# Attention scores of the later batches: three float16 products of split operands instead of one float32 product

## The chip, the cores and the metric

The kernel runs on one core of one Trainium2 chip. Its time is what the device takes for one execution, in microseconds (us). The core has TensorE for matrix products (in the profile PE, and PEld for its weight loads), VectorE (DVE), ScalarE (ACT), GpSimd (POOL) and SyncE (SP, which here only issues transfers). They run side by side, each through its own list of instructions in a fixed order, and wait for each other by semaphores.

## The reference

Windowed attention with 32 global tokens, and behind it a feed-forward layer on all 4608 tokens. Cut to what matters:

```python
# batch 8, heads 8, 512 local and 32 global tokens, head size 64
s_g = scale * q_g @ concat(k_g, k_l).T            # global queries see every key
s_ll = where(abs(i - j) <= 32, scale * q_l @ k_l.T, -1e9)
a_l = softmax(concat(scale * q_l @ k_g.T, s_ll))  # softmax subtracts the row's maximum
out = concat(softmax(s_g) @ v, a_l @ v)           # v = concat(v_g, v_l)
x = out.transpose(0, 2, 1, 3).reshape(4608, 512)
h = x @ w_in                                      # 512 x 2048
return (h * tanh(softplus(h))) @ w_out            # 2048 x 512
```

All inputs and outputs are float32. The queries and keys are drawn with a spread of about 0.57 to 0.8.

## The kernel before

**Attention.** The 8 heads of a batch are handled as 4 pairs; a pair's two heads stand on partitions 0 to 63 and 64 to 127. One transfer brings a pair's tile `qk` (128 x 1344 float32): 512 query columns, and 832 key columns in which each of four blocks of 128 queries finds its own keys, its neighbours' edge keys and the 32 global keys side by side. A unit is (batch b, pair hp, query block t); 128 units run in order. `scores` (L727) makes the scores of two units at once, one matrix product for each unit and head, into two of the three PSUM buffers of ring `sc`: this document calls that a score group, and there are 64 of them, 8 in each batch. For the second pair of every two it adds the global queries' scores of both pairs (`qg`, L744, and `g_go`, L886 to L891, in the third `sc` buffer). From batch 2 on all of this is one group, which this document calls a large one: 2 of the 8 groups in a batch. `row_max` (L760) masks a unit's scores, scales them and takes the row maximum on VectorE, `expo` (L767) takes the exponential on ScalarE; then the probabilities are split into float16 high and low parts (`ph`), turned by transposing transfers (`pt`), and multiplied with the values (`pv`, L856, into `U`).

**Feed-forward.** The tokens go through in 17 blocks of up to 256. All its products are already three float16 products of high and low parts. Blocks 0 to 4 use plain products (`m1_mm` into the two PSUM buffers of ring `h`, `mish` on ScalarE, `g_hi` and `g_lo`, then `m2_mm` into `o`). Blocks 5 and later form the first layer from seven products of sums instead of eight (`st_step`, L1158); for it `s_make` (L1074 and L1097) builds sums of weights on VectorE once, in the time of the batches 1 to 3, through a scratch tile `t`.

**What sets the order.** Every step is a task with the engines it may run on, a duration, and the tiles it reads and writes. The class `Plan` plays the program through with these durations and then writes each engine's instructions in the order of its start times; a task with two possible engines goes to the one that takes it first. So a change of a duration, a tile or a constant moves instructions on all engines. `slot(u)` names the tasks around unit u: scores of unit u+1, probabilities of u, values of u-1 or u-2, and the feed-forward steps due at u (table `S1`).

**Tiles.** `qk` has four buffers for the batches 0 and 1 and two afterwards; when they are free, buffer 3 also holds the scratch `t`, and parts of the others take sums of weights.

Of the kernel before, what the change touches and what calls it, by code (L numbers as in the profile page):

```python
# [10 lines left out]
F32 = mybir.dt.float32  # L11
# [27 lines left out]
MASKED = -8.0e9  # L39
# [13 lines left out]
T2 = 128  # L53
T3 = 131
T4 = 135
QTWO = 2
VPOOL = 1

# [257 lines left out]
def attn_mish_kernel(ctx: ExitStack, tc: tile.TileContext, qk, vm, vg, qg, w1, w2, consts_in, out, w64):  # L316
# [23 lines left out]
    def rings(pool, *table):  # L340
        for tag, bufs, shape, dt in table:
# [5 lines left out]
          ("vgraw", 1, [128, 128], F32), ("qg", 2, [128, HP, 64], F32),  # L347
# [6 lines left out]
          ("wm", 2, [128, 1], F32), ("dg", 2, [128, 128], F32), ("dv", 1, [128, 128], F32), ("pg", 1, [128, 2], F32), ("c", 3, [128, 3], F32),  # L354
# [34 lines left out]
    QK = own("qk", 4, [128, SL + KW], F32, (QTWO * HP, 2))  # L389
# [10 lines left out]
    pl.ring("t", 1, lambda name, i: QK[3][:, :512], keys={0: ("qk", 3)})  # L400
# [319 lines left out]
    HALVED = 2  # L720
# [39 lines left out]
    def row_max(b, hp, t, h):  # L760
# [3 lines left out]
            out=half(P, h, w), in0=X[s][:, cols(t)], in1=mask[:, m0:m0 + w], scale=-SCALE, scalar=3.0e38, op0=ALU.add, op1=ALU.min,  # L764
            accum_out=X[nm]), r=[s, "consts"], w=[[P, h]] if h else (), new=[("nm", nm)] if h else [("P", P), ("nm", nm)])
# [134 lines left out]
    def g_max(b, hp):  # L900
# [870 lines left out]
```

## Time and profile before

| | |
|---|---|
| time, median of 3 runs (lowest, highest) | 895.84 us (894.86, 897.37) |
| the profiled execution's own time | 897.46 us |
| its span, first to last instruction | 895.7 us |
| PE busy | 864.5 us, 97% of the span |
| DVE busy | 703.5 us, 79% |
| ACT busy | 584.0 us, 65% |
| POOL busy | 118.3 us, 13% |

The span is what the trace covers; 1.8 us of the profiled time lie around it. An engine is busy while an instruction of it is in progress, so an engine with a share near 100% has no time left, and one with a lower share waits or has nothing to do. Scores of the batches 0 and 1 start before 205.4 us, those of batch 2 at 205.44, of batch 3 at 274.85, of batch 4 at 353.55; the last score group is at 722.42 us. What follows is feed-forward alone.

### The profile page before, as it was taken

The numbers are of one execution on the slowest core, as the hardware profiler recorded it, in microseconds if no ns is written. First come the engines' busy times: TensorE is split into PE (matmuls) and PEld (weight loads), VectorE is DVE, ScalarE is ACT, GpSimd is POOL, SyncE is SP. The second block draws the span as 40 slices with busy tenths as digits, with TensorE's granted clock in tenths as the row PEclk, the third lists the DMA queues.
The fourth block names the chain that finished last, engine by engine and source line by source line (L and its number), as shares of the span: only waits on it lengthen the run. The fifth ranks groups of instructions, "written<-read, shape, count | busy, mean of one in ns | idle before, by whom it ended". The sixth has DMA issues, their size and how long they took to land.

```text
span 895.7 us, 24348 instructions
## 1 busy us (share of the span) xinstructions
PE 864.5 (97%) x9844; PEld 640.0 (71%) x9844; DVE 703.5 (79%) x1806; ACT 584.0 (65%) x1297; POOL 118.3 (13%) x224
## 2 busy tenths in 40 slices
PE   2889999999999999999999999999999999999997
PEld 1657668676676767777777777677777777689996
DVE  6999967559999797888659765886569789987675
ACT  2677887458688876786557665666567665454442
POOL 6211320021023102111110201011111000000000
PEclk9999999999999999999999999999999999999999
DMA  9975236634896976687637663666645431000000
GB/s 364 354 251 181 62 82 119 124 88 90 168 207 117 192 121 150 130 152 119 136 79 143 111 169 61 135 138 122 116 98 114 84 75 37 1 25 2 25 26 25
DMA packets 194593, 107.26 MB, mean 120 GB/s; under 512 B 175024, under 2 KB 179440, under 8 KB 193456
## 3 DMA queue, kind: packets, MB, share of 16 engines
q1 hardware_dynamic: 184352, 83.61, 44.2%
q0 software_dynamic: 9264, 19.21, 7.3%
q10 hardware_dynamic: 864, 2.88, 0.9%
q8 instruction: 77, 1.26, 0.6%
q14 instruction: 36, 0.29, 0.1%
HBM read 49.04 MB, written 8.91 MB: 65 GB/s over the span
## 4 chain that ended last, share of the span: by engine, by line
PE 87%; DVE 8%; DMA 3%; ACT 1%; issue 0%; POOL 0%; DVEq 0%; SPq 0%; ACTq 0%
PE o L1253 32%; PE h L1158 24%; PE h L989 10%; PE s L740 6%; PE U L856 5%; PE o L1348 4%; DMA pt<-ph 2%; DVE W L554 2%; DMA vraw<-in_vm 2%; DVE W L552 1%; PE gu L940 1%; PE g L891 1%; DVE W L545 1%; DVE P L763 1%; PE hx L1348 1%; DVE vmx L638 1%
## 5 line engine op out<-in xcount | busy, mean ns | idle before, releaser
L1253 PE MATMUL o<-W,G 128*128 128x512 f16 x1344 | 314.3, 379 | 0.0
L1253 PEld LDWEIGHTS <-G 128*128 128x128 f16 x1344 | 123.3, 97 | 127.2 <-issue 2.0
L1158 PEld LDWEIGHTS <-W 128*128 128x128 f16 x2880 | 167.5, 98 | 17.6 <-issue 2.2
L772 ACT ACTIVATE P<-P,nm 128x192 f32<-128x192 f32 (+1 forms) x256 | 117.7, 461 | 28.9 <-DVE nm L763 28.4
L989 PE MATMUL h<-xh,W 128*128 128x256 f16 x640 | 113.2, 273 | 1.0 <-ACT EE L1035 1.0
L763 DVE CUSTOM_DVE_ANT_0 P<-s,consts 128x192 f32<-128x192 f32 (+1 forms) x256 | 88.7, 368 | 32.1 <-PE s L740 28.9
L989 PEld LDWEIGHTS <-W 128*128 128x128 f16 x960 | 91.6, 98 | 16.9 <-issue 3.9
L1158 PE MATMUL h<-xh,W 128*128 128x128 f16 x1056 | 96.0, 219 | 0.0
L1158 PE MATMUL h<-xl,W 128*128 128x128 f16 x528 | 90.8, 219 | 0.0
L989 PE MATMUL h<-xl,W 128*128 128x256 f16 x320 | 87.2, 272 | 0.0
L712 POOL DMA_DIRECT2D vc<-vf x81 | 41.5, 515 | 256.3 <-DVE vf L694 115.0
L789 DVE SCALAR_TENSOR_TENSOR ph<-P,ph 128x384 f16<-128x384 f32 (+1 forms) x112 | 65.4, 587 | 11.0 <-ACT ph L456 10.0
L1158 PE MATMUL h<-raw,W 128*128 128x128 f16 x1152 | 73.9, 219 | 0.0
L856 PEld LDWEIGHTS <-pt 128*128 128x128 f16 (+1 forms) x1536 | 59.8, 98 | 18.1 <-issue 7.3
L740 PE MATMUL s<-qk 64*128 64x192 f32 (+1 forms) x512 | 63.8, 369 | 0.0
L449 ACT COPY EE<-h 128x512 f32<-128x512 f32 x48 | 28.0, 582 | 48.2 <-PE h L1158 45.3
L456 ACT ACTIVATE ph<-P 128x448 f16<-128x448 f32 (+1 forms) x102 | 54.8, 543 | 5.2 <-DMA pt<-ph 4.9
L1187 ACT ACTIVATE EE<-EE,c 128x1024 f32<-128x1024 f32 x24 | 27.6, 1149 | 46.1 <-DVE EE L1184 46.1
L856 PE MATMUL U<-vc,pt 96*128 96x64 f16 x768 | 56.0, 192 | 0.0
L856 PE MATMUL U<-vf,pt 128*128 128x64 f16 x720 | 52.4, 193 | 0.8 <-DMA pt<-ph 0.8
L740 PEld LDWEIGHTS s<-qk 64*128 64x128 f32 x512 | 42.8, 190 | 10.8 <-issue 5.5
L458 DVE TENSOR_SCALAR G<-VX,c 128x1024 f16<-128x1024 f32 x24 | 18.1, 754 | 38.7 <-ACT VX L1187 38.7
(246 smaller groups left out, 1583.7 us busy)
## 6 DMA issues: line engine op xcount, KB each, us to landing
qk<-in_qk SPq DMA_DIRECT2D x32, 672.0 KB, 4.9
W<-in_w POOLq DMA_DIRECT2D x17, 512.0 KB, 7.6
out<-ob SPq DMA_DIRECT2D x33, 256.0 KB, 2.8
vraw<-in_vm SPq DMA_DIRECT2D x8, 1024.0 KB, 6.1
raw<-in_w POOLq DMA_DIRECT2D x10, 512.0 KB, 5.2
W<-in_w ACTq DMA_DIRECT2D x5, 512.0 KB, 7.8
pt<-ph SPq DMA_TRANSPOSE x112, 3.4
vc<-vgf POOLq DMA_DIRECT2D x28, 48.0 KB, 3.0
```

The costliest lines, as they stand in the source:

```text
L449: A.copy(dst, src)
L456: A.activation(out=dst, in_=src, func=AF.Copy, scale=c)
L712: stream(POOL, dma(kib), lambda: G.dma_start(dst(), src()), 512, r=[r], w=[w], new=new, table="dma")
L740: T.matmul(X[s[h]][:, cols(u)], X[qk][r, u * 128:(u + 1) * 128], X[qk][r, SL + OWN[u]:SL + OWN[u] + WIDTH[u]], start=True, stop=True)
L763: pl.add(DVE, 77 + 1.03 * w, lambda: V.tensor_tensor_reduce(out=half(P, h, w), in0=X[s][:, cols(t)], in1=mask[:, m0:m0 + w], scale=-SCALE, ...
L772: pl.add(ACT, 460, lambda: A.activation(out=half(P, h, w), in_=half(P, h, w), func=AF.Exp, bias=X[nm], scale=-1.0, accum_out=X[sums][:, t, ...
L789: pl.add(DVE, dve(n), lambda: V.scalar_tensor_tensor(p_part(X[ph], t, 1), p_src(X[P], t), PSC, p_part(X[ph], t, 0), ALU.mult, ALU.subtract ...
L856: T.matmul(X[u][:, t, h, :], X[pt][:k, p * 4 + (c * 2 + h if b < TURNED else h * 2 + c), :], X[vx][:k, t, vl, h * 64:(h + 1) * 64], start= ...
L989: T.matmul(X[h][:, f * TB:(f + 1) * TB], wh(i, wl)[:, off:off + 128], X[x][:, d, o:o + TB], start=(n == 0), stop=(n == 11))
L1158: T.matmul(X[h][:, c:c + 128], form(J + jj, wl)[:, off:off + 128], x(l, d), start=(p in (1, 2, 5) and c == 0 and n == 0), stop=(n == 5), s ...
L1253: T.matmul(X[o], gp(g, blk, i)[:, f, t * 128:(t + 1) * 128], wh(8 + i, wl)[:, f * 512:(f + 1) * 512], start=(turn == 0 and n == 0), stop=( ...
L1348: T.matmul(X[o][:, cols], a_form(a, jj, f), b_form(w, jj, f), start=(fresh and n == 0), stop=(n == 11), skip_group_check=True)
```

## The change

From batch 2 on (`HALVED = 2`) the scores, the global ones too, are made from float16 parts.

- The global queries move into the tile `qk`, which grows from 1344 to 1408 columns; the separate transfer and tile `qg` go.
- Each pair's `qk` tile of batches 2 to 7 lands in one single buffer (QK[0]). `qk_scale` adds up the absolute values along each partition of the query side (576 columns) and of the key side (832 columns) with two ScalarE passes into `qs`; then GpSimd takes the maximum over the partitions, and five small VectorE instructions make powers of two from it (`sq`). `qk_split` writes the scaled high parts (ScalarE or VectorE, whichever the plan finds free) and the low parts (VectorE) as float16 into a new tile `pa`, two buffers in the places of QK[1] and QK[3]. The three steps are named 5, 4 and 3 units ahead of the pair's first scores.
- A score group of two units is now 3 products (high x high, high x low, low x high) for each unit and head: 12 float16 matrix products with 12 weight loads, where there were 4 float32 ones. A large group adds 6 for the global keys and 12 for the local keys, where there were 2 and 4.
- The scale is taken back in `row_max` and, through a small tile `cg`, in the global softmax.
- `t` becomes a tile of its own; constants of the plan differ.

```diff
-MASKED = -8.0e9
+MASKED = -1.0e30
+QG = 64
+KO = SL + QG
+QTOP, QTINY = 2.0 ** 14, 2.0 ** -14
...
-T2 = 128
-T3 = 131
+T2 = 127
+T3 = 133
...
-QTWO = 2
+HALVED = 2
...
+KLOAD, KSCALE, KSPLIT = 5, 4, 3
...
-    QK = own("qk", 4, [128, SL + KW], F32, (QTWO * HP, 2))
+    QK = own("qk", 4, [128, KO + KW], F32, (HALVED * HP, 1))
...
-    pl.ring("t", 1, lambda name, i: QK[3][:, :512], keys={0: ("qk", 3)})
+    ts_ = own("t", 1, [128, 512], F32, None)
+    pl.ring("dv", 1, lambda name, i: ts_[0][:, :128], keys={0: ("t", 0)})
+    pl.ring("pa", 2, lambda name, i: halfwords(QK[2 * i + 1]).rearrange("p (a c) -> p a c", a=2), keys={0: ("qk", 1), 1: ("qk", 3)})
...
-    def g_load(b):
-        stream(DMA, dma(128), lambda: load(X["qg", b], qg[b]), 1024, new=[("qg", ("qg", b))])
...
+    SIDES = (slice(0, KO), slice(KO, KO + KW))
+
+    def qk_scale(b, hp):
+
+        k, p, m, q, s = ("qk", b, hp), ("pa", b, hp), ("qs", b, hp), ("q2", b, hp), ("sq", b, hp)
+        for i, c in enumerate(SIDES):
+            pl.add(ACT, act(c.stop - c.start) + 90, lambda i=i, c=c: A.activation(out=X[p][:, 0, c].bitcast(BF16), in_=X[k][:, c], func=AF.Abs, bias=0.0, scale=1.0,
+                                                                    accum_out=X[m][:, i:i + 1]),
+                   r=[k], w=[[m, i], [p, i]] if i else (), new=() if i else [("qs", m), ("pa", p)])
+        pl.add(POOL, 900, lambda: G.partition_all_reduce(X[q], X[m], 128, RED.max), r=[m], new=[("q2", q)])
+
+        def go():
+            x, y = X[q], X[s]
+            V.tensor_scalar(x, x, QTINY, 1.0 / QTOP, ALU.max, ALU.mult)
+            pow2(x)
+            V.reciprocal(y[:, 0:2], x)
+            V.scalar_tensor_tensor(y[:, 2:3], x[:, 0:1], -SCALE, x[:, 1:2], ALU.mult, ALU.mult)
+            V.tensor_scalar(y[:, 3:4], y[:, 2:3], -1.0, None, ALU.mult)
+        pl.add(DVE, 420, go, w=[q], new=[("sq", s)])
+
+    def qk_split(b, hp):
+        k, p, s = ("qk", b, hp), ("pa", b, hp), ("sq", b, hp)
+        for i, c in enumerate(SIDES):
+            n = c.stop - c.start
+            pl.add([(ACT, act(n)), (DVE, dve2(n))], 0, lambda e, i=i, c=c: scaled(e, X[p][:, 0, c], X[k][:, c], X[s][:, i:i + 1]), r=[k, s], w=[[p, i]])
+        for i, c in enumerate(SIDES):
+            pl.add(DVE, dve(c.stop - c.start), lambda i=i, c=c: V.scalar_tensor_tensor(X[p][:, 1, c], X[k][:, c], X[s][:, i:i + 1], X[p][:, 0, c], ALU.mult, ALU.subtract),
+                   r=[k, s, [p, i]], w=[[p, (i, 1)]])
+
+    THREE = ((0, 0), (0, 1), (1, 0))
...
+        three = THREE if b >= HALVED else (None,)
+        part = lambda b, hp, i: X["pa", b, hp][:, i] if i is not None else X["qk", b, hp]
+
         def go():
             for u in (t, t + 1):
-                for h in range(2):
-                    r = slice(h * 64, h * 64 + 64)
-                    T.matmul(X[s[h]][:, cols(u)], X[qk][r, u * 128:(u + 1) * 128], X[qk][r, SL + OWN[u]:SL + OWN[u] + WIDTH[u]],
-                             start=True, stop=True)
+                for n, x in enumerate(three):
+                    i, j = x or (None, None)
+                    for h in range(2):
+                        r = slice(h * 64, h * 64 + 64)
+                        T.matmul(X[s[h]][:, cols(u)], part(b, hp, i)[r, u * 128:(u + 1) * 128], part(b, hp, j)[r, KO + OWN[u]:KO + OWN[u] + WIDTH[u]],
+                                 start=n == 0, stop=n == len(three) - 1)
...
+            for m, x in enumerate(three):
+                i, j = x or (None, None)
+                for n in range(2):
+                    T.matmul(X[g][n * 64:n * 64 + 64, c * 256:c * 256 + 256], part(n, i)[:, SL:KO], loc(part(n, j), 2 * c), start=m == 0, stop=m == len(three) - 1)
...
-    BLK2 = 18.779
+    BLK2 = 22.636
...
-    LAGX = 16.978
+    LAGX = 18.906
...
-    PACE = 0.821
-    MORE = 2.517
+    PACE = 0.895
+    MORE = 1.553
...
-    LATER = 28
-    BOOST = 21.993
-    BOOST2 = -10.661
+    LATER = 27
+    BOOST = 12.408
+    BOOST2 = 0.356
...
+        if KSPLIT in ready:
+            qk_split(*ready[KSPLIT][:2])
+        if KSCALE in ready:
+            qk_scale(*ready[KSCALE][:2])
...
-        if load3 and t == 0:
-            qk_load(*n3)
+        if KLOAD in ready:
+            qk_load(*ready[KLOAD][:2])
```

Three places in the order of instructions. In the names, `s_2_2_0_0` is batch 2, pair 2, first two units, head 0; `nm` is a row maximum, `U_2_1` the values' product of pair 1, `h_3_2` chunk 2 of the first feed-forward layer in block 3.

TensorE at the score groups of batch 2, pairs 2 and 3, before the change:

```order
L740 MATMUL s_2_2_0_0_3253<-qk0_103 128x192
...
L856 MATMUL U_2_1_3165<-vf1_118,pt1_123 128x64
...
L989 MATMUL h_3_1_3198<-xh_1_1798,W_73 128x256
...
L989 MATMUL h_3_2_3295<-xh_1_1798,W_73 128x256
...
L740 MATMUL s_2_2_1_0_3315<-qk0_103 128x224
...
L740 MATMUL s_2_3_0_0_3438<-qk1_104 128x192
```

and with it:

```order
L779 MATMUL s_2_2_0_0_3376<-qk1_104 128x192
...
L898 MATMUL U_2_1_3317<-vf1_118,pt1_124 128x64
...
L779 MATMUL s_2_2_1_0_3422<-qk1_104 128x224
...
L898 MATMUL U_2_1_3317<-vf1_118,pt2_125 128x64
...
L779 MATMUL s_2_3_0_0_3482<-qk3_106 128x192
...
L936 MATMUL g_2_3_3484<-qk1_104 64x256
...
L1044 MATMUL h_3_2_3547<-xh_1_1826,W_73 128x256
```

Before, feed-forward chunks stand between the score groups; now three score groups follow each other with only products of values between them, and the next chunk (`h_3_2`) comes behind all three.

ScalarE at the same place, with the change:

```order
L814 ACTIVATE P1_76,sums_2_2_3401<-P1_76,nm_2_2_0_0_3396 128x192
...
L463 ACTIVATE qk3_106<-qk0_103,sq_2_3_3336 128x832
L814 ACTIVATE P2_77,sums_2_2_3401<-P2_77,nm_2_2_1_1_3439 128x224
...
L814 ACTIVATE P1_76,sums_2_2_3401<-P1_76,nm_2_2_3_1_3478 128x192
L463 ACTIVATE ph1_82<-P2_77 128x2x224
L1090 ACT_TABLE_LOAD
L1090 ACTIVATE EE_120<-h_3_0_3222,c_3_1982 128x512
```

The mish of chunk `h_3_0`, which frees the PSUM buffer that `h_3_2` needs, now stands behind all eight exponentials of pair 2 and a high part; before the change it stood ahead of them.

VectorE there, with the change:

```order
L805 ISA P2_77,nm_2_2_1_0_3418<-s_2_2_0_0_3376,consts_65,sq_2_2_3146 128x224
...
L1129 TENSOR_TENSOR t0_121<-t0_121,W_73 128x512
L831 SCALAR_TENSOR_TENSOR ph1_82<-P0_75,ph1_82 128x2x192
L805 ISA P2_77,nm_2_2_1_1_3439<-s_2_2_0_1_3377,consts_65,sq_2_2_3146 128x224
...
L805 ISA P0_75,nm_2_2_2_1_3461<-s_2_2_1_1_3423,consts_65,sq_2_2_3146 128x224
...
L703 SCALAR_TENSOR_TENSOR qk3_106<-qk0_103,sq_2_3_3336,qk3_106 128x832
...
L805 ISA P1_76,nm_2_2_3_1_3478<-s_2_2_1_1_3423,consts_65,sq_2_2_3146 128x192
```

The low part of the next pair's keys (L703, 832 columns) and sums of weights (L1129) now stand between the row maxima of pair 2. Of the 48 steps of L1074 (now L1129) 4 stood ahead of batch 2, 26 in it and 18 behind it; with the change 22, 17 and 9.

## Rows read from the trace of the kernel before

**Rows 1.** The page: the span, and the engines' busy time (share) and instructions.

```profile
span 895.7 us, 24348 instructions
PE 864.5 (97%) x9844; PEld 640.0 (71%) x9844; DVE 703.5 (79%) x1806; ACT 584.0 (65%) x1297; POOL 118.3 (13%) x224
```

**Rows 2.** Windows cut at batch starts: length, busy us of each engine (instructions), clock, DMA.

```profile
0.00:108.65 108.65, 85.00 (x739) 59.47 (x739) 98.04 (x272) 72.75 (x182) 34.78 (x62) 0.97 0.70 247
108.65:205.44 96.79, 96.60 (x906) 69.15 (x905) 63.22 (x190) 67.17 (x153) 12.68 (x25) 1.00 0.49 100
205.44:274.85 69.41, 69.41 (x695) 46.30 (x694) 66.69 (x188) 53.65 (x129) 11.53 (x22) 1.00 0.79 164
274.85:353.55 78.70, 78.06 (x823) 55.53 (x820) 68.04 (x192) 60.35 (x138) 10.40 (x21) 1.00 0.75 144
353.55:445.24 91.69, 91.69 (x1220) 69.19 (x1217) 70.78 (x191) 69.07 (x151) 17.74 (x36) 1.00 0.72 136
...
542.01:638.78 96.77, 96.77 (x1206) 70.13 (x1204) 69.62 (x191) 62.17 (x142) 12.81 (x25) 1.00 0.62 120
```

**Rows 3.** Timeline of PE around a plain score group: start us, us, instruction, count.

```profile
406.44 0.97 PE L740 MATMUL s<-qk 64*128 64x224 f32 x8
407.34 0.34 PE L1158 MATMUL h<-raw,qk 128*128 128x128 f16 x3
```

**Rows 4.** Timeline of PE around a large score group.

```profile
222.74 0.97 PE L740 MATMUL s<-qk 64*128 64x192 f32 x8
223.65 0.31 PE L744 MATMUL s<-qk,qg 128*64 128x32 f32 x4
223.78 1.06 PE L891 MATMUL g<-qk,qg 128*64 128x256 f32 x8
224.78 0.61 PE L1253 MATMUL o<-W,G 128*128 128x512 f16 x2
```

**Rows 5.** Timeline of PE, float16 products in a row.

```profile
410.39 2.75 PE L1253 MATMUL o<-W,G 128*128 128x512 f16 x12
412.98 1.50 PE L1158 MATMUL h<-raw,G 128*128 128x128 f16 x24
414.32 0.25 PE L856 MATMUL U<-vf,pt 128*128 128x64 f16 x3
```

**Rows 6.** Timeline of PE, one float32 record on the whole array.

```profile
52.27 0.59 PE L609 MATMUL rest<-W,dg 128*128 128x512 f32 x1
52.70 0.38 PE L610 MATMUL rest<-W,minus 128*128 128x512 f16 x1
```

**Rows 7.** Timeline of PEld: weight loads.

```profile
404.64 0.45 PEld L856 LDWEIGHTS <-pt 128*128 128x128 f16 x12
405.02 0.99 PEld L1253 LDWEIGHTS <-G 128*128 128x128 f16 x6
```

**Rows 8.** Groups of instructions: busy us, mean ns of one, idle before.

```profile
L1048 DVE SCALAR_TENSOR_TENSOR G<-EE,c,G 128x512 f16<-128x512 f32 x40 | 29.8, 748 | 0.5
L1196 DVE SCALAR_TENSOR_TENSOR G<-VX,c,G 128x1024 f16<-128x1024 f32 x24 | 30.7, 1280 | 0.4
L864 DVE TENSOR_SCALAR rs<-sums 128x8 f32<-128x8 f32 (+1 forms) x40 | 6.5, 165 | 3.4 <-ACT P L772 3.2
L456 ACT ACTIVATE vf<-vraw,sv 128x512 f16<-128x512 f32 x29 | 20.5, 714 | 0.4
L456 ACT ACTIVATE W<-W,sw 128x1024 f16<-128x1024 f32 x15 | 17.2, 1144 | 1.3 <-DVE W L615 1.2
L772 ACT ACTIVATION_READ_ACCUMULATOR P<-P,nm 128x1 f32 x256 | 48.1, 188 | 0.0
L1074 DVE TENSOR_TENSOR qk<-qk,W 128x512 f32<-128x512 f32 (+1 forms) x28 | 19.2, 685 | 0.2
```

**Rows 9.** Waits of one GpSimd transfer: total us, times, longest.

```profile
POOL vgg L712 <- PE gu L940: 128.3, 7, 42.2
```

**Rows 10.** Transfers: KB each, median us from issue to landing.

```profile
qk<-in_qk SPq DMA_DIRECT2D x32, 672.0 KB, 4.9
```

More of the change, by code (lines that the diff above doesn't have):

```diff
@@ L748, in scores @@
         one = both and b >= HALVED
-        pl.add(PE, 1970 if one else 1145 if both else 907, go, r=[qk] + ([("qg", b), ("qk", b, hp - 1)] if both else []),
+        tag = "pa" if b >= HALVED else "qk"
+        pl.add(PE, 1330 if one else 545 if b >= HALVED else 1145 if both else 907, go, r=[(tag, b, hp)] + ([(tag, b, hp - 1)] if both else []),
                new=[("sc", s[0]), ("sc", s[1])] + ([("sc", ("g", b, hp))] if one else []))
@@ L887, in g_go @@
     def g_go(b, hp):
-        q, g, k = ("qg", b), ("g", b, hp), [("qk", b, hp - 1 + n) for n in range(2)]
+        g, three = ("g", b, hp), THREE if b >= HALVED else (None,)
+        part = lambda n, i: X["pa", b, hp - 1 + n][:, i] if i is not None else X["qk", b, hp - 1 + n]
         for c in range(2):
-            for n in range(2):
-                T.matmul(X[g][n * 64:n * 64 + 64, c * 256:c * 256 + 256], X[q][:, hp - 1 + n, :], loc(X[k[n]], 2 * c), start=True, stop=True)
+            for m, x in enumerate(three):
+                i, j = x or (None, None)
+                for n in range(2):
+                    T.matmul(X[g][n * 64:n * 64 + 64, c * 256:c * 256 + 256], part(n, i)[:, SL:KO], loc(part(n, j), 2 * c), start=m == 0, stop=m == len(three) - 1)
     def g_scores(b, hp):
-        pl.add(PE, 1017, lambda: g_go(b, hp), r=[("qg", b)] + [("qk", b, hp - 1 + n) for n in range(2)], new=[("sc", ("g", b, hp))])
+        pl.add(PE, 1017, lambda: g_go(b, hp), r=[("qk", b, hp - 1 + n) for n in range(2)], new=[("sc", ("g", b, hp))])
     def g_rest(b, hp):
@@ L1478, in attn_mish_kernel @@
     NEXT1 = 4
-    NEXT2 = 17
+    NEXT2 = 18
     NU = B * 16
@@ L1504, in attn_mish_kernel @@
     splits = []
-    F0 = 41.356
-    FSTEP = 0.782
+    F0 = 41.301
+    FSTEP = 0.862
     SFREE = S1[(GLATE - 1) * NF + 4]
     forms = [(F0 + FSTEP * n, (n // 3, n % 3 + 1)) for n in range(12)]
-    forms = [(max(k, SFREE + 1 if PIECES[j * 3 + n - 1][0][0] == "G" else 16 * QTWO + 1 if PIECES[j * 3 + n - 1][0][0] == "qk" else 0), (j, n)) for k, (j, n) in forms]
+    forms = [(max(k, SFREE + 1 if PIECES[j * 3 + n - 1][0][0] == "G" else 16 * HALVED + 1 if PIECES[j * 3 + n - 1][0][0] == "qk" else 0), (j, n)) for k, (j, n) in forms]
     forms += [(S1[ST0 * NF - 4 + j] + 1, (j, 4)) for j in range(4)]
@@ L1534, in slot @@
         b, hp, t = bu if bu else (0, 0, -1)
-        n1, n3 = divmod(b * HP + hp + 1, HP), divmod(b * HP + hp + 1, HP)
-        load3 = bu and b >= HALVED and n3 > (HALVED, 3 if QTWO > HALVED else 1) and n3[0] < B
+        n1 = divmod(b * HP + hp + 1, HP)
+        ready = {k: x for k in (KLOAD, KSCALE, KSPLIT) for x in [unit(u + k)] if x and x[0] >= HALVED and x[2] == 0}
         mv1 = bu and b >= HALVED and n1[0] < B
```

60 lines of the change are left out of this document (32 added, 28 removed).

## The prediction

> **What bounds the kernel now.** I read the page's busy shares first: PE works in 97% of the span, and no other engine above 79% [rows 1]. That is a mean over stages, so I cut the span at the starts of the batches and read every engine in each window [rows 2]. In the first 108.65 us PE is idle for 23.7, while DVE works for 98.0. From there to the end of batch 6 PE has no gap to speak of: 96.60 of 96.79 us, 69.41 of 69.41, 78.06 of 78.70, then all. So in the 48 score groups that the change touches PE is the bound, and a microsecond taken from its list is one gained, as long as the others keep up. The same windows say how near they are. In batch 2 DVE is busy for 66.69 of 69.41 us (96%), in batch 3 for 68.04 of 78.70, in batch 4 for 70.78 of 91.69, in batch 6 for 69.62 of 96.77. ACT has 15.8 us free in batch 2 and 35 in batch 6. The batches that follow each other fastest have the least room, and the change gives every pair more work on DVE and ACT.
>
> **Taken from PE.** A plain group lasts 0.90 us (406.44 to 407.34) for 8 records of 192 and 224 columns [rows 3]. Float16 products of 512 columns follow each other every 0.216 us and those of 128 columns every 0.056 [rows 5], a line of 0.003 us plus 0.417 ns per column: 0.083 us for 192 columns, 0.096 for 224, 0.109 for 256. A float32 record of 512 columns took 0.43 us, two such passes [rows 6]; a float32 product is two records, so four passes. One head's passes come to 4 x (0.083 + 0.096) = 0.715 us, two heads one after the other to 1.43. The measured 0.90 lies below that, so the heads, each on its half of the rows, run side by side, and 0.185 us are filling and switching. With three passes, 3 x 0.179 = 0.537. If all of the 0.185 stays the group lasts 0.72 and the gain is 0.18; if none stays, 0.36. I take 0.12 of it, near three quarters: 0.66 us, a gain of 0.24.
>
> A large group is 0.91 + 0.13 + 1.00 = 2.04 us [rows 4]. The middle becomes about 0.10. The last part is 16 passes of 256 columns, 8 behind each other if two run side by side (0.87), plus 0.13; now 6 x 0.109 + 0.13 = 0.78. Sum 0.66 + 0.10 + 0.78 = 1.54, gain 0.50 (0.41 to 0.77 by the same two ends). Batches 2 to 7 have 36 plain and 12 large groups: 36 x 0.24 + 12 x 0.50 = **14.6 us off PE** (11.4 to 22.2), 2.4 in each batch.
>
> **More weight loads.** A plain group now has 12 loads. Where float16 products are short, loads start 0.032 us apart, though each shows about 0.1 us (12 from 404.64, the twelfth ending 0.45 later) [rows 7]: they overlap, 12 x 0.032 = 0.38 lies below 0.537, and I add nothing. The Trainium skill ("TensorE: Matmul & The Clock Gate", section "LDWEIGHTS (loading the stationary operand)") prices a load at columns / 1.2 ns, 107 ns for 128 columns; one behind the other, 12 would take an estimated 1.28 us and the group would be longer than today. The trace disagrees for loads on the whole array; no row shows float16 loads for one half of it, so loads in single file stay a rival below.
>
> **Added to ACT and DVE.** For each of 24 pairs ACT sums absolute values over 576 and 832 columns. By its rows (512 columns 714 ns, 1024 columns 1144 ns, reading a sum 188 ns [rows 8]) that is 0.77 + 0.98 + 2 x 0.188 = 2.1 us; the high parts are 1.75 where ACT makes them, as it does in 43 of 48. 3.7 us a pair. DVE forms the low parts, between its rows of 512 and 1024 columns (748 and 1280 ns [rows 8]) 0.81 + 1.08 = 1.9, and the scales, five small instructions at 165 ns [rows 8], 0.8: 2.7 us a pair. The small copy `cg`, one a pair, is inside these.
>
> In batches 4 to 7 this is hidden. Batch 6: PE 96.8 - 2.4 = 94.4 us, DVE 69.6 + 10.8 = 80.4, ACT 62.2 + 14.8 = 77.0. Batch 4: PE 89.3, DVE 81.6, ACT 83.9. Batch 3 has PE 76.3, ACT 75.2, and DVE 70, since there 8 sums of weights fewer (0.685 each [rows 8]) and one pair's low parts fewer weigh against the added work. That is tight; I take 0, with a bound in the rivals.
>
> **Where it is not hidden.** In batch 2 PE needs 69.4 - 2.4 = 67.0. DVE gets 66.7 + 5 x 2.7 (its own four pairs' parts and one made ahead) + 2.2 (low parts that now stand there), less 13 sums of weights (8.9) that the order moves ahead of batch 2, into a window where DVE is busy for only 63.2 of 96.8 us [rows 2]: 73.4. That is 6.4 more than PE has, if DVE never waits, and 9.5 at the 96% that it reached. The order shows where: three score groups with only values' products between them, the chunk `h_3_2` behind, whose PSUM buffer is freed by a mish that ACT does only after all exponentials of that pair and a high part, and those wait for row maxima with a low part and weight sums between them. I take a **stall of 8 us** in batch 2 (bounds 0, if PE's order leaves enough between, and 12.8, from 73.4 at 92%). ACT there needs 53.7 + 14.8 = 68.5, close behind DVE.
>
> **Waits and transfers.** The maximum over partitions stands in POOL's list, behind moves that wait for PE (128.3 us in 7 waits, the longest 42.2 [rows 9]). It is named four units ahead, about 17 us in batch 2, and the pair's scores would wait behind a late one. One landing buffer serves all pairs: transfer 4.9 us [rows 10], sums 2.1, maximum and scales about 1.4 (an estimate), high 1.75, low 1.9, 12.1 us in a row, against 69.4 / 4 = 17.4 us for a pair in batch 2 and 24 in batch 6. It fits, with less slack in batch 2. On SP the next load waits until the low part is done, with the transposes of `pt` queued behind it; that is part of the 8. The bytes loaded stay the same (704 KB a pair for 672, and no `qg`). The start and the feed-forward tail behind the last group have the same work; 0, by 2 or 3 either way.
>
> **Sum.** 897.5 (the profiled execution's own time) - 14.6 + 8 = 890.9, 6.6 less. The profiled execution lies 1.6 above the median of the runs, so against 895.84: **889 us**.
>
> **Rivals.** About 0.3%, 2.7 us, is what a measurement of this kernel can tell from no change.
> - *Forecast* (0.47): 884 to 893, stall of 3 to 12.
> - *Nothing stalls, or the groups come near pure passes* (0.18): 895.8 less 14.6 to 20, 876 to 882. For it: ACT and DVE have free time in all batches from 4 on, and early steps of batch 2 could slip ahead. Against: 73.4 against 67.0.
> - *The stalls eat the saving* (0.19): 12 to 17 us of stall in batches 2 and 3, 893.2 to 898.5. For it: batch 3's ACT at 75.2 of 76.3.
> - *DVE and ACT become the bound* (0.13), the case on the other side: they wait for each other in a chain (maximum, exponential, high, low), so neither fills its time. At 92%: batch 2 lasts 73.4 / 0.92 = 79.8 (12.8 over PE), batch 3 75.2 / 0.92 = 81.7 (5.4), batch 4 83.9 / 0.92 = 91.2 (1.9): 20.1 less 14.6 is 5.5 slower, 901. It decides when these stalls pass 17.3 us, at a fill of about 93%. For it: ACT never worked over 77% of a batch when DVE was at 96%. Against: DVE did reach 96%, with PE never idle.
> - *Weight loads in single file* (0.03): 12 x 0.10 + 0.12 = 1.32 us a plain group, 0.42 more than now (36 x 0.42 = 15); a large one has 30 loads, 3.0 us, 1.0 more (12): 895.8 + 27 without any stall, 923 or later. The Trainium skill's price for a load, named above, would bring about this.
>
> **Range and chances.** 877 to 901 takes in the forecast, most of the first rival, all of the second and half of the third. Faster by over 0.3%: the forecast and the first, 0.65. Within: 0.19. Slower: 0.13 + 0.03 = 0.16. The forecast's own range is 884 to 893.
>
> **What would show it.** In the changed profile: plain groups of 0.66 us and large ones of 1.54 (the PE term); PE idle in batch 2 by about 8 us, around pairs 2 and 3, with waits of `h` chunks for the mish and of row maxima in DVE's list behind; DVE over 92% there; in batches 4 to 7 PE without gaps, and each some 2.4 us shorter; ACT up by about 80 us in all and DVE by 65. Wrong would be: a group of 0.9 us or more (loads), idle PE in batch 4 or later (ACT, or a late maximum on POOL), scores waiting for `pa` (the landing chain), or a changed tail.

## The result and the profile after

The changed kernel takes 905.56 us (904.16 to 906.78, 4 runs) where the kernel before took 896.12 (894.86 to 897.37): ratio 1.0105, 95% interval 1.0083 to 1.0127. It is 9.4 us slower; 6.6 us faster was forecast. The profiled execution took 904.16.

The page of the changed kernel, span and busy time, beside [rows 1]:

```profile
span 902.3 us, 25249 instructions
PE 856.3 (95%) x10108; PEld 633.3 (70%) x10108; DVE 766.9 (85%) x1987; ACT 657.2 (73%) x1446; POOL 125.1 (14%) x248
```

PE is busy for 8.2 us less and the span is 6.6 longer, so its idle time grew by 14.8: 2.8 of it before batch 2, 11.7 in batches 2 to 4. Windows of the changed kernel, cut at the batch starts as in [rows 2] (the first two are batches 0 and 1; an engine's idle time is the length less its busy time):

```profile
0.00:98.27 98.27, 71.67 (x648) 50.37 (x648) 87.11 (x253) 64.63 (x172) 27.16 (x51) 1.00 0.75 267
98.27:207.38 109.11, 109.11 (x1008) 77.26 (x1008) 86.86 (x233) 78.94 (x180) 19.30 (x39) 1.00 0.45 91
207.38:287.58 80.20, 71.76 (x740) 48.82 (x740) 73.29 (x216) 66.14 (x153) 12.27 (x25) 0.91 0.76 146
287.58:370.42 82.84, 79.88 (x904) 56.73 (x902) 71.24 (x204) 66.82 (x153) 13.15 (x26) 0.98 0.68 131
370.42:460.91 90.49, 89.50 (x1227) 66.35 (x1226) 82.61 (x230) 81.88 (x179) 16.86 (x34) 1.00 0.74 140
460.91:555.32 94.41, 94.35 (x1249) 68.25 (x1249) 79.48 (x212) 76.24 (x168) 13.52 (x28) 1.00 0.64 126
555.32:650.12 94.80, 94.67 (x1250) 68.34 (x1250) 81.57 (x230) 76.84 (x170) 14.50 (x30) 1.00 0.61 125
```

Stage by stage in us, with the forecast's own terms:

| | batches 0, 1 | 2 | 3 | 4 | 5 | 6 | 7 and tail | span |
|---|---|---|---|---|---|---|---|---|
| before | 205.4 | 69.4 | 78.7 | 91.7 | 96.8 | 96.8 | 256.9 | 895.7 |
| forecast | 205.4 | 75.0 | 76.3 | 89.3 | 94.4 | 94.4 | 254.5 | 889.3 |
| after | 207.4 | 80.2 | 82.8 | 90.5 | 94.4 | 94.8 | 252.2 | 902.3 |

From batch 4 on the forecast holds to 1.2 us a batch. Batch 2 is 5.2 longer than forecast, batch 3 is 6.5, the start 2.0; batch 7 and the tail are 2.3 shorter. Some of this is work that the new order moved: PE's list in batch 3 now holds 12 more products into `o`, 48 more of 128 columns and 24 fewer of 256, at the intervals of the prediction an estimated 2.7 us more, and behind batch 6 there are 11 products into `o` fewer.

PE at a plain and at a large score group of the changed kernel in undisturbed batches, beside [rows 3, 4]:

```profile
508.25 0.71 PE L779 MATMUL s<-qk 64*128 64x192 f16 x12
508.89 0.26 PE L898 MATMUL U<-vf,pt 128*128 128x64 f16 x3
...
529.62 0.71 PE L779 MATMUL s<-qk 64*128 64x192 f16 x12
530.26 0.27 PE L785 MATMUL s<-qk 128*64 128x32 f16 x6
530.37 0.82 PE L936 MATMUL g<-qk 128*64 128x256 f16 x12
531.13 0.26 PE L898 MATMUL U<-vf,pt 128*128 128x64 f16 x3
```

From start to start a plain group takes 0.64 us (0.66 forecast), a large one 0.64 + 0.11 + 0.76 = 1.51 (1.54 forecast).

PE in batch 2 of the changed kernel, rows with idle time (in brackets, with what ended it) and two of a chunk:

```profile
244.08 0.71 PE L779 MATMUL s<-qk 64*128 64x192 f16 x12
245.28 0.26 PE L898 MATMUL U<-vf,pt 128*128 128x64 f16 x3 [0.50 <-DMA pt<-ph]
...
247.46 0.25 PE L779 MATMUL s<-qk 64*128 64x224 f16 x1 [1.64 <-ACT xg L463]
248.98 1.19 PE L779 MATMUL s<-qk 64*128 64x224 f16 x11 [1.27 <-DVE nm L805]
...
254.36 1.20 PE L779 MATMUL s<-qk 64*128 64x192 f16 x11 [2.90 <-DVE nm L805]
...
258.35 0.37 PE L1044 MATMUL h<-xh,W 128*128 128x256 f16 x1 [0.46 <-ACT EE L1090]
...
258.73 0.63 PE L1044 MATMUL h<-xh,W 128*128 128x256 f16 x2
...
262.31 0.38 PE L1044 MATMUL h<-xh,W 128*128 128x256 f16 x2
...
267.34 0.27 PE L1044 MATMUL h<-xh,W 128*128 128x256 f16 x1 [1.46 <-ACT EE L1090]
```

This is the place that the orders ahead of the prediction show: three score groups, only products with values between them, the chunk behind them. The same two products of a chunk take 0.63 us at 258.73 and 0.38 at 262.31: from 248.4 to 262.0, behind the first waits, the granted clock is at the lower of its two levels, 1.2 GHz (0.50 in this window):

```profile
248.40:262.00 13.60, 9.45 (x83) 6.74 (x83) 13.57 (x40) 10.47 (x26) 2.54 (x5) 0.50 0.81 185
```

PE's 9.45 us of work there would be some 4.7 at full clock (an estimate: half). ScalarE ahead of the last wait:

```profile
261.87 1.28 ACT L683 ACT_TABLE_LOAD   x1 [1.49 <-DMA qk<-in_qk]
263.17 0.68 ACT L683 ACTIVATE qk<-qk 128x576 bf16<-128x576 f32 x1
263.76 0.19 ACT L683 ACTIVATION_READ_ACCUMULATOR qk<-qk 128x1 f32 x1
263.85 0.88 ACT L683 ACTIVATE qk<-qk 128x832 bf16<-128x832 f32 x1
264.63 0.19 ACT L683 ACTIVATION_READ_ACCUMULATOR qk<-qk 128x1 f32 x1
264.73 0.56 ACT L463 ACTIVATE ph<-P 128x448 f16<-128x448 f32 x1
265.31 1.28 ACT L1090 ACT_TABLE_LOAD   x1
```

The pass of absolute values waits for its transfer (issued at 253.40, landed after 8.4 us), loads a table, and the mish that PE waits for stands behind both and a second table load.

### The profile page after: what moved, and what is told of

Read it like the earlier page. It is cut to its first block, busy times and chain, and to the rows that moved or that the text cites. A ratio compares the mean times of both kernels' runs of the same rounds, so it can differ in the third digit from the quotient of the medians.

```text
span 902.3 us, 25249 instructions
## 1 busy us (share of the span) xinstructions
PE 856.3 (95%) x10108; PEld 633.3 (70%) x10108; DVE 766.9 (85%) x1987; ACT 657.2 (73%) x1446; POOL 125.1 (14%) x248
## 4 chain that ended last, share of the span: by engine, by line
PE 66%; DVE 17%; ACT 7%; issue 4%; DMA 4%; POOL 0%; DVEq 0%; SPq 0%; ACTq 0%; POOLq 0%
PE o L1308 25%; PE h L1213 17%; PE h L1044 9%; PE o L1403 4%; PE U L898 4%; PE s L779 3%; DVE P L805 2%; DMA vraw<-in_vm 2%; DVE W L561 1%; DMA xh<-xs 1%; DVE W L559 1%; ACT qk L683 1%; ACT L683 1%; DVE W L552 1%; PE gu L995 1%
## 5 line engine op out<-in xcount | busy, mean ns | idle before, releaser
L1044 PE MATMUL h<-xh,W 128*128 128x256 f16 x640 | 116.9, 277 | 4.6 <-ACT EE L1090 4.6
L805 DVE CUSTOM_DVE_ANT_0 P<-s,consts,sq 128x192 f32<-128x192 f32 (+1 forms) x192 | 79.3, 428 | 10.7 <-PE s L779 10.5
L831 DVE SCALAR_TENSOR_TENSOR ph<-P,ph 128x448 f16<-128x448 f32 (+1 forms) x112 | 64.3, 585 | 13.1 <-ACT ph L463 12.2
L779 PE MATMUL s<-qk 64*128 64x192 f16 (+3 forms) x704 | 54.6, 283 | 7.5 <-DVE nm L805 5.6
L814 ACT ACTIVATION_READ_ACCUMULATOR P<-P,nm 128x1 f32 x256 | 48.2, 188 | 0.0
L686 POOL PARTITION_ALL_REDUCE q<-qs x24 | 9.7, 405 | 271.6 <-ACT qk L683 271.6
L703 DVE SCALAR_TENSOR_TENSOR qk<-qk,sq,qk 128x576 f16<-128x576 f32 (+1 forms) x48 | 45.2, 946 | 0.1
```

The lines of the kernel that those rows point to most:

```text
L703: pl.add(DVE, dve(c.stop - c.start), lambda i=i, c=c: V.scalar_tensor_tensor(X[p][:, 1, c], X[k][:, c], X[s][:, i:i + 1], X[p][:, 0, c], A ...
L779: T.matmul(X[s[h]][:, cols(u)], part(b, hp, i)[r, u * 128:(u + 1) * 128], part(b, hp, j)[r, KO + OWN[u]:KO + OWN[u] + WIDTH[u]], start=n = ...
L805: pl.add(DVE, 77 + 1.03 * w, lambda: V.tensor_tensor_reduce(out=half(P, h, w), in0=X[s][:, cols(t)], in1=mask[:, m0:m0 + w], scale=X["sq", ...
L814: pl.add(ACT, 460, lambda: A.activation(out=half(P, h, w), in_=half(P, h, w), func=AF.Exp, bias=X[nm], scale=-1.0, accum_out=X[sums][:, t, ...
L831: pl.add(DVE, dve(n), lambda: V.scalar_tensor_tensor(p_part(X[ph], t, 1), p_src(X[P], t), PSC, p_part(X[ph], t, 0), ALU.mult, ALU.subtract ...
L1044: T.matmul(X[h][:, f * TB:(f + 1) * TB], wh(i, wl)[:, off:off + 128], X[x][:, d, o:o + TB], start=(n == 0), stop=(n == 11))
```

## The experiments

The runs test theories of what PE waits for. Theory A says that the work added to VectorE and ScalarE fills them in batches 2 to 4. Theory B blames the plan's constants and the tiles, theory C the places of the small new steps and the single landing buffer. Later came A' (one stretch of VectorE's list is overfull), D (the lower clock after the waits costs time of its own) and O (the order of the same work in the lists).

**Work taken out, order kept.** These kernels keep every list of the changed kernel and leave out part of the work. `abs8` sums absolute values over 8 columns only:

```diff
-X[p][:, 0, c].bitcast(BF16), in_=X[k][:, c]
+X[p][:, 0, c.start:c.start + 8].bitcast(BF16), in_=X[k][:, c.start:c.start + 8]
```

> The changed kernel with its order of instructions kept on every engine, but each of the two passes of absolute values reads 8 columns in place of 576 and 832 (the scales are then no bounds). ScalarE has some 1.2 us less per pair, 28 us in all; the table loads, the all-reduce and the wait for the transfer stay. Theory A (the work added to VectorE and ScalarE fills the batches 2 to 4, and PE waits for it): the two waits of PE for the mish in batches 2 and 3 (1.46 and 2.72 us) shrink to about 2 us together, the rest stays: 901 to 904 us against 905.6. Theory B (the changed constants and tiles of the plan cost the time, whatever the splitting takes): no change, 905 to 906. Theory C (what costs is where the small new steps stand in the lists and what they wait for, not how long they last): no change, 905.

`lo8` forms the low parts of 8 columns only, and the products read the high parts in their place (`i and 0`, `j and 0` for `i`, `j`):

```diff
-V.scalar_tensor_tensor(X[p][:, 1, c], X[k][:, c], ...
+V.scalar_tensor_tensor(X[p][:, 1, c.start:c.start + 8], X[k][:, c.start:c.start + 8], ...
```

> The changed kernel with its order kept, but each low part is formed for 8 columns in place of 576 and 832, and the products read the high parts in its place, in equal number and size. VectorE has some 1.6 us less per pair, 8 us in batch 2. Theory A: VectorE's row maxima come earlier, PE's idle time in batch 2 falls from 8.4 to 1 to 3 us and its slow clock there goes: 894 to 899 us. Theory B: 905. Theory C: 903 to 905, since the low parts wait for the same things at the same places.

`abslo8` has both edits:

> Both together: passes of absolute values and low parts on 8 columns, order kept. Theory A: PE is idle for less than 3 us in the batches 2 to 4, and the saving on PE shows: 888 to 894 us, below the kernel before. Theory B: 905. Theory C: 902 to 905.

`lit` puts the literal back in place of the pair's scale in the row maximum:

```diff
-scale=X["sq", b, hp][:, 2:3] if b >= HALVED else -SCALE
+scale=-SCALE
```

> The changed kernel with its order kept, but the row maximum multiplies by a literal as before the change, in place of the pair's scale read from a tile (so the scores are scaled wrongly). The maxima of the batches 2 to 7 took 412 and 445 ns against 351 and 385; 60 ns on 192 of them are 11.5 us on VectorE, 1.9 in each batch. Theory A: durations return to 351 and 385, and batches 2 and 3 give back 2 to 4 us: 901.5 to 903.5. Theories B and C: 905 to 906.

Measured, as ratios to the kernel before: abs8 1.0014 (1.0004 to 1.0023), lo8 1.0026 (1.0011 to 1.0042), abslo8 0.9980 (0.9967 to 0.9994), lit 1.0043 (1.0028 to 1.0058). All four take time off (the changed kernel once more, below, is 1.0094): abs8 and lit as much as A says or more, lo8 and abslo8 less. But batch 2 stays. Its windows in lo8 and abslo8:

```profile
207.67:287.39 79.72, 72.19 (x739) 49.16 (x739) 67.96 (x217) 65.73 (x153) 12.31 (x25) 0.91 0.77 146
...
207.85:287.87 80.02, 70.87 (x741) 48.63 (x740) 67.90 (x217) 61.15 (x152) 12.02 (x25) 0.94 0.72 145
```

VectorE has 5.3 us less, is busy for 85% of the batch, and PE idles for 7.5 and 9.2 us, where A had 3 at most. The batch's amount of work, A, does not explain its idle time.

**Constants, tiles and the first float16 batch.** `again` is the changed kernel once more, the measure for the other runs.

> The changed kernel once more, unaltered, beside the others of this call: 904 to 907 us, 1.008 to 1.013 of the kernel before by every theory; it is the measure for the three below and for the runs with shortened steps.

1.0094 (1.0071 to 1.0117). In its profile batch 2 lasted 82.2 us with 8.9 of idle PE (80.2 and 8.4 before): differences of 1 or 2 us in one profile mean little. `oldc` sets back 15 constants:

```diff
-    BLK2 = 22.636
+    BLK2 = 18.779
...
-    BOOST = 12.408
+    BOOST = 21.993
```

> The changed kernel with the 15 constants of the plan that the change altered (due times of feed-forward steps, sums and loads) set back to their values before; the splits, the float16 products and the tiles stay, and the plan orders anew. Shortened splits left 7.5 to 9.2 us of idle PE in batch 2, so the amount of work is not all. Theory A (the added work fills VectorE and ScalarE): 903 to 908, and 7 us or more of idle PE in batch 2. Theory B (the constants and tiles cost it: they put the feed-forward chunks out of the place where PE would need them): 886 to 893, idle PE below 3 us in batch 2. Theory C (the new small steps wait in the lists, above all for a late transfer into the single landing buffer): 898 to 904, with idle PE behind that transfer.

1.0442 (1.0414 to 1.0470), above every number, with 7.5 us of idle PE in batch 2. B falls as the cause of the stall: without its constants the change costs 4%. `F8` and `F4` put the batch from which scores are float16 into a number of its own:

```diff
+FROM = 4
...
-three = THREE if b >= HALVED else (None,)
+three = THREE if b >= FROM else (None,)
```

> The changed kernel without float16 scores: all batches make float32 scores from a ring of two landing buffers as before the change, with no sums, scales and splits; the constants, the wider tile and the separate scratch tile are those of the change. Theory A: as before the change, 0.998 to 1.003 of its time. Theory B: idle PE in batch 2 as with the change, 1.008 or more. Theory C: 0.998 to 1.003.

1.0028 (1.0016 to 1.0040): constants and tiles alone cost 2.5 us. Its profile is longer at the start (209.7 us to batch 2 against 205.4) and in batch 3 (81.5 against 78.7) and 3.0 shorter behind batch 6, where it too has 11 products into `o` fewer; batch 2 has no idle PE.

> Float16 scores from batch 4 on; batches 2 and 3 make float32 scores from two landing buffers as before the change; all else as changed. In the changed kernel the batches 5 to 7 were 2.0 to 2.4 us shorter than before, so four such batches give 8 to 9, less 1 to 2 for the first splits, which fall into batch 3. Theory A: 888 to 891 us, 0.991 to 0.994. Theory B: batch 2 keeps its stall, 896 to 900. Theory C: 889 to 893, for the transfer of batch 4 finds more room.

1.0001 (0.9986 to 1.0015): a time that B gave, but not in its way. Batches 2 and 4 of F4:

```profile
209.41:279.42 70.01, 70.01 (x689) 47.20 (x688) 58.51 (x176) 55.76 (x130) 10.46 (x21) 1.00 0.76 158
...
361.18:457.21 96.03, 90.05 (x1226) 66.06 (x1225) 84.94 (x232) 77.10 (x172) 15.33 (x30) 1.00 0.65 134
```

With the splits gone batch 2 has no idle PE; 6.0 us came up in the first float16 batch, in waits for five other steps, the longest 1.7 us.

**One stretch, the clock, a later start.** `sum8` shortens two of the three steps of each sum of weights to 8 columns:

```diff
-V.tensor_tensor(X[ts], x(), y(), how)
+V.tensor_tensor(X[ts][:, :512 if first else 8], x()[:, :512 if first else 8], y()[:, :512 if first else 8], how)
```

> The changed kernel with its order kept, but of the three steps of each sum of weights only the first works on 512 columns, the other two on 8 (so the sums are incomplete). VectorE has some 6 us less in batch 2, most of it between 240 and 258 us, where it never stood still in the changed kernel nor in the run with shortened sums of absolute values and low parts. Theory A' (not the batch, but this stretch of VectorE's list is overfull: sums of weights, splits and row maxima together; PE's three score groups there wait for the maxima): idle PE in batch 2 falls from 8.4 to 3 to 5 us, 899 to 902 us, 1.002 to 1.005 of the kernel before. Theory C (the single landing buffer, its late transfer and the chain behind it hold the mish, and that PE): 7 us or more of idle PE stay, 1.007 or more.

1.0081 (1.0052 to 1.0109), 7.4 us of idle PE. `thin` has the edits of sum8, abs8 and lo8:

> Sums of weights, passes of absolute values and low parts all shortened, order kept; VectorE has about 14 us less in batch 2. Theory A': only the wait behind the late transfer (1.5 to 2.4 us) and little else is left of PE's idle time in batch 2, 2 to 3.5 us: 886 to 891, 0.988 to 0.993. Theory C: 6 us or more stay, 0.995 or more.

0.9971 (0.9957 to 0.9985). Its batches 2 and 5:

```profile
207.91:284.82 76.91, 69.27 (x739) 47.69 (x738) 62.33 (x217) 61.03 (x152) 11.90 (x25) 0.96 0.77 150
...
455.01:549.15 94.14, 94.14 (x1249) 68.19 (x1248) 74.63 (x211) 72.59 (x170) 14.89 (x29) 1.00 0.61 126
```

VectorE is down by 11 us, to 81% of the batch; the batch is 3.3 us shorter, and 7.6 us of idle PE remain. So A' does not explain the idle time either. In sum thin takes 1.2% from the changed kernel, more than the whole loss: the added work has its price, 3.3 us in batch 2 and 3.1 in batches 3 and 4 by the profiles, but little of it is idle time of PE (10.6 us in batches 2 to 4, against 12.4). `fill` makes four sets of products with values, ahead of the long waits, several times over:

```diff
-            for h in range(2):
+            for h in list(range(2)) * AGAIN.get((b, hp, t), 1):
```

> The changed kernel with the same lists, but four sets of products with the values in batch 2, which stand ahead of the long waits, are made 5, 9, 2 and 5 times over (17 extra sets of 12 products, 6.0 us at full clock; the result is the same). Theory D (beside the 8.4 us of idle PE, batch 2 lost some 4.5 us because the clock was at half after the idle stretches, as products at twice the interval show): with PE kept at work the products run at the full interval, the extra sets lie in time that was idle, and the time falls by 2 to 4.5 us against the changed kernel: 1.004 to 1.007. If the slow products had cost nothing, because what comes next waits anyway: no change or up to 2 us more, 1.009 to 1.012.

1.0092 (1.0073 to 1.0111), no change. Its batch 2 has a clock of 0.98, 75.0 us of busy PE (an estimated 6.0 of them extra) and the same length, 80.2. What PE lost to the lower clock it would have waited for otherwise: D falls as a cause of its own. `F5` is F4 with `FROM = 5`:

> Float16 scores from batch 5 on only; the batches 2 to 4 make float32 scores from two landing buffers. The run with float32 scores throughout and the constants of the change was 1.0028; each steady float16 batch gives 2.0 to 2.4 us back. Theory A': sums of weights and splits no longer meet, three batches give 6 to 7 us: 890 to 893, 0.993 to 0.996. Theory C: the first float16 batch stalls wherever it is (as with batch 4 first, where PE was idle for 6 us): 0.998 to 1.002.

1.0004 (0.9991 to 1.0017), a time that C gave; but its stall in the first float16 batch is not there: batches 5 and 6 took 95.3 and 96.0 us, with 0.8 and 1.3 us of idle PE. This run decides nothing.

**The order of the same work.** `dur` alters one planned duration:

```diff
-        pl.add(DVE, 77 + 1.03 * w, lambda: V.tensor_tensor_reduce(
+        pl.add(DVE, (137 if b >= HALVED else 77) + 1.03 * w, lambda: V.tensor_tensor_reduce(
```

> The changed kernel with one number altered: the plan counts 60 ns more for a row maximum from batch 2 on, which is what it took. Work and tiles stay; the order of the instructions from batch 2 on becomes another. Theory O (the idle time of PE in batches 2 to 4 is set by the order, by where feed-forward chunks and the mish stand between the score groups): idle time and total move by more than 5 us, and here, where the chunks stand still further apart, up: 910 to 920, 1.013 to 1.025. Theory A (the amount of work on VectorE and ScalarE): same work, 904 to 908.

1.0217 (1.0198 to 1.0236); idle PE 14.1, 3.0 and 4.2 us in batches 2 to 4. The waits of batch 2 are other ones than before, 9.2 us of them behind transposing transfers (`pt`, `gpt`). `ord2` has this edit and 22 other numbers of the plan:

```diff
-    BLK2 = 22.636
+    BLK2 = 28.344
...
-    PACE = 0.895
+    PACE = 0.993
```

> As dur, with other due times for feed-forward steps, sums of weights and loads (17 numbers of the plan). The same work from batch 2 on, in another order in all batches. Theory O: PE is idle for 3 to 8 us in batches 2 to 4 together, against 12.4 in the changed kernel, and the time is 889 to 897, 0.991 to 0.999. Theory A: 904 to 908, idle time as in the changed kernel.

1.0057 (1.0041 to 1.0073). Idle PE 2.5, 7.2 and 0.1. One number of the plan and a set of them move the time by some 11 us up and 3 down with the work unchanged: O, though ord2 fell short of its numbers. The three score groups of batch 2 that follow each other in the changed kernel are in ord2:

```profile
241.25 0.71 PE L779 MATMUL s<-qk 64*128 64x192 f16 x12
241.90 2.76 PE L1308 MATMUL o<-W,G 128*128 128x512 f16 x12
...
244.85 1.46 PE L1308 MATMUL o<-W,G 128*128 128x512 f16 x6
246.25 0.71 PE L779 MATMUL s<-qk 64*128 64x224 f16 x12
246.89 0.28 PE L1044 MATMUL h<-xh,W 128*128 128x256 f16 x1
...
253.15 0.63 PE L779 MATMUL s<-qk 64*128 64x192 f16 x10 [0.30 <-DVE qk L703]
```

Feed-forward work stands between them again. The stretch from the first of them to PE's first product behind the last wait there, in the changed kernel, in thin and in ord2, and ord2's whole batch 2:

```profile
244.08:258.35 14.27, 7.29 (x94) 5.26 (x92) 14.07 (x46) 12.05 (x30) 2.54 (x5) 0.65 0.68 182
```

```profile
244.60:256.75 12.15, 6.59 (x93) 4.92 (x91) 10.79 (x44) 11.14 (x29) 2.54 (x5) 0.72 0.75 204
```

```profile
241.25:256.14 14.89, 13.56 (x159) 9.53 (x157) 14.16 (x42) 13.44 (x34) 2.78 (x6) 1.00 0.77 196
205.83:283.52 77.69, 75.20 (x799) 51.72 (x799) 74.16 (x220) 70.62 (x158) 12.30 (x26) 1.00 0.70 147
```

The stretch is about as long in ord2 as in the changed kernel, and VectorE is busy for as much of it (14.2 and 14.1 us); but PE has 13.6 us of work in it and not 7.3. In thin VectorE has 3.3 us less there, and the stretch is 2.1 shorter. So in the changed kernel its length follows VectorE and ScalarE, and how much of it PE idles depends on what PE's own list holds there. `ord4` (on F4) and `ord8` (on F8) have other due times too, among them

```diff
-    BLK2 = 22.636
+    BLK2 = 4.062
...
-    BOOST2 = 0.356
+    BOOST2 = 17.100
```

> Float16 scores from batch 4 on, as in F4 (1.0001), with other numbers in the plan (17 due times, and the 60 ns). Theory O: the 6 us of idle PE in batch 4 go, four batches give 2.6 us each: 884 to 890, 0.985 to 0.992. Theory A: batch 4's idle time stays, 895 to 899.

1.0021 (1.0012 to 1.0030), a time that A gave. Batch 4's idle time did fall, from 6.0 to 1.7 us, but batches 5 to 7, which had 0.6 at most in the changed kernel, now have 2.9, 3.0 and 1.9, above all for `o` behind ScalarE's copy `ob`.

`ord8` has, among others, `BLK2 = 26.010` and `BOOST2 = 17.622`:

> Float32 scores in all batches, as in F8 (1.0028), with other numbers in the plan, as control for ord4: what a better order is worth without float16. All theories: 894 to 899, 0.996 to 1.002; what ord4 lies below it is what float16 products give in four batches, 8 to 11 us if nothing stalls.

1.0066 (1.0041 to 1.0092), slower than F8, so no control for ord4; this run decides nothing.

`thinshort` adds to thin a shorter transfer:

```diff
-load(X["qk", b, hp], qk[b, hp])
+load(X["qk", b, hp][:, :128 if b >= HALVED else KO + KW], qk[b, hp][:, :128 if b >= HALVED else KO + KW])
```

> As thin (sums of weights, passes of absolute values and low parts shortened, order of the changed kernel), and each pair's transfer from batch 2 on brings 128 of the 1408 columns (64 KB in place of 704; the rest is what stood there). Theory C, the landing buffer: most of the 7.6 us of idle PE in batch 2 of thin go, 2 us or less stay; 884 to 889, 0.985 to 0.990. Theory O, the order: only the wait behind the late transfer goes (2.07 us of the 7.6), 5 to 6 us stay, because the three score groups still stand together in PE's list and each waits for the maxima and exponentials of the one before; 890 to 893, 0.992 to 0.995.

0.9963 (0.9951 to 0.9976), above both numbers, but the waits decide: batch 2 keeps 5.6 us of idle PE, as O has it. PE's waits in thin, then in thinshort:

```profile
246.87 0.25 PE L779 MATMUL s<-qk 64*128 64x224 f16 x1 [1.09 <-ACT xg L463]
...
250.33 0.31 PE L779 MATMUL s<-qk 64*128 64x192 f16 x1 [1.39 <-ACT qk L463]
252.26 1.20 PE L779 MATMUL s<-qk 64*128 64x192 f16 x11 [1.62 <-DVE nm L805]
...
264.58 0.27 PE L1044 MATMUL h<-xh,W 128*128 128x256 f16 x1 [2.07 <-ACT EE L1090]
```

```profile
247.03 0.25 PE L779 MATMUL s<-qk 64*128 64x224 f16 x1 [1.09 <-ACT xg L463]
...
250.50 0.32 PE L779 MATMUL s<-qk 64*128 64x192 f16 x1 [1.39 <-ACT qk L463]
252.44 1.20 PE L779 MATMUL s<-qk 64*128 64x192 f16 x11 [1.62 <-DVE nm L805]
```

The wait behind the transfer is gone, the others are the same to 0.01 us. `ord4m` is ord4 with `T1` to `T4` and this number set back to those of the changed kernel:

```diff
-    BOOST2 = 17.100
+    BOOST2 = 0.356
```

> Float16 scores from batch 4 on, the numbers of the plan as in ord4, but BOOST2 and T1 to T4, which act from batch 4 on, as in the changed kernel, whose batches 5 and 6 lasted 94.4 and 94.8 us with less than 0.2 us of idle PE (ord4: 96.4 and 99.3, with 2.9 and 3.0). Theory O: batches 0 to 4 as in ord4 (444 us), the idle time of batches 5 to 7 goes, 6 to 8 us: 890 to 893, 0.991 to 0.995. Theory A: ScalarE has the same work as in ord4, so the batches 5 to 7 keep their idle time, 897 to 900.

889.72 us, 0.9922 (0.9907 to 0.9937): the fastest of all, by 7 us against the kernel before. Batches 2 to 5 of ord4m:

```profile
207.50:273.64 66.14, 66.14 (x671) 45.44 (x671) 56.99 (x171) 52.27 (x126) 8.65 (x17) 1.00 0.83 161
273.64:355.84 82.20, 82.20 (x878) 58.30 (x876) 67.74 (x194) 61.94 (x143) 15.52 (x32) 1.00 0.75 143
355.84:445.71 89.87, 89.58 (x1226) 66.25 (x1225) 81.49 (x228) 76.90 (x172) 16.28 (x31) 1.00 0.64 134
445.71:540.46 94.75, 94.31 (x1249) 68.26 (x1248) 79.49 (x221) 74.89 (x168) 14.24 (x29) 1.00 0.65 127
```

Batch 4, the first with float16 scores, has VectorE at 91% and 0.3 us of idle PE: a VectorE as full as in the changed kernel's batch 2 need not stall PE.

## Why the prediction was wrong

- **The saving on PE was right.** 0.26 and 0.53 us a group (0.24 and 0.50 forecast) make 2.6 us a batch; in thin, whose later batches have no waits, batch 5 lasts 94.1 us against 96.8. That is 15.7 in all for 14.6.
- **Loads in single file: refuted.** A group of 12 loads lasts 0.64 us. By the price of a load in the Trainium skill ("TensorE: Matmul & The Clock Gate", section "LDWEIGHTS (loading the stationary operand)") its loads alone would take an estimated 1.28; the trace disagrees for half the rows as well.
- **The step that failed is "Where it is not hidden".** Its place was right, and PE idled for 8.4 us against 8. But the batch lasted 80.2 us and not 75.0, and the stall was priced from sums over the batch, VectorE's 73.4 against PE's 67.0, which do not set it: thin takes 11 us from the first, to less than the second, and keeps 7.6 us of idle PE. So the 8 is in part luck. What the runs showed in its place is the stretch of three groups: with no chunk between them PE goes at the pace of a chain (scale, high part, the global queries' scaled result `xg`, maximum, exponential) through lists in fixed order, 14.3 us for 7.3 of its own work; with chunks between them, in ord2, it has work for 13.6 of 14.9. And the batch lost more than its idle time: 80.2 - 67.0 = 13.2 us, some 4.8 beyond the idle 8.4, at the lower clock. fill shows that this is no separate loss that more work on PE would give back.
- **That the sum itself came out (73.4, measured 73.3) is luck as well.** It takes off 13 sums of weights (8.9 us); by the counts ahead of the prediction 9 left the batch, 6.2 us by the trace. The row maxima took 2.0 us more, which it had not priced. Other steps made up for both. In batch 3 its terms add up to some 71.4 us for VectorE, where it says 70 (71.2 measured).
- **"That is tight; I take 0" was the other step.** Batch 3 lasted 82.8 us for 76.3. An estimated 2.7 of the 6.5 is the work moved there (F8, with constants and tiles alone, is 2.8 longer than before in this batch). Idle PE is 3.0 (0.6 before), 2.7 of it one wait for a mish behind a pass of absolute values and two table loads. The clock behind it was lower, 0.98 over the batch; about 1.5 us are left for that, which is not measured by itself. VectorE filled 86% of the batch, ScalarE 81%.
- **"The start and the feed-forward tail ... have the same work; 0" was off by parts.** To batch 2 the changed kernel took 2.0 us more, with 2.8 more of idle PE; batch 7 and the tail were 2.3 shorter than forecast, by the work that had moved ahead. That the two cancel is luck.
- **The rival on the other side gave the sign and nearly the time** (79.8, 81.7 and 91.2 us for batches 2 to 4; 80.2, 82.8 and 90.5 measured; 901 against 905.6). Its chain is what the stretch shows, with VectorE busy for 14.1 of 14.3 us. But it bound the whole batch by VectorE's fill of 92%, and ord2 filled VectorE to 95% of batch 2 with 2.5 us of idle PE; and batch 3 came near its number by work moved and table loads. In sum the 12.4 us of idle time in batches 2 to 4 and the slow products around it (4.8 and about 1.5) came to more than the 15.7 saved, and the start added 2.8 of idle time; constants and tiles alone, without float16, cost 2.5 (F8).
- **Not priced:** a row maximum that reads its scale from a tile takes 412 and 445 ns against 351 and 385 before; 192 of them are 11.5 us on VectorE. lit gave 0.5% back.

What stays open: which links of the chain could be moved to let float16 start in batch 2 without loss; no order tried here had less than 9.8 us of idle PE in batches 2 to 4 with the splits there (ord2, with 7.2 of them in batch 3), and whether one exists was not settled. How much of the 9.4 us is the added work and how much the order was not separated either: work taken out (thin) and an order changed (dur) each move the time by 11 us. With the start in batch 4, float16's share in ord4m's 7 us was not separated from that of its order.

## What to carry to other kernels

Where a scheduler rewrites every list, price a stall stretch by stretch: how long the chain through the other engines takes there, less the work that stands in the waiting engine's list between its two ends. The busy sums of a whole batch do not give it: here 11 us off VectorE moved the idle time by 1 us, and one number of the plan moved the total by 11. A change that saves on the bound and adds steps elsewhere belongs first where the bound has work to put between (batch 4 here, not batch 2), with an order made anew for it.

## What was not expected of the hardware

Of the 24 first passes of absolute values 14 began with a table load (18.0 us in all, 1.28 each), where the Trainium skill ("ScalarE: Activation LUTs", section "Table sets: the hidden batching unit") counts abs among the functions of every set; this kernel's program loads one all the same. A pair's transfer issued 1.4 us behind the values' transfer took 8.4 us to land, against a median of 4.9. PE's granted clock was 0.50 for 13.6 us (0.91 over batch 2) in a batch whose waits were only 0.2 to 2.9 us long; two products of a chunk then took 0.63 us for 0.38.
